# Loading half of the queries and keys through GpSimd's DMA queue, with the conversion to float16 on the way

## The chip, the core and the metric

The kernel runs on one core of one Trainium2 chip. The metric is the device time of one execution in microseconds (us); lower is better. TensorE (PE in the profile) multiplies matrices into PSUM; VectorE (DVE), ScalarE (ACT) and GpSimd (POOL) do the elementwise work; SyncE (SP) only issues transfers. ScalarE and GpSimd can issue transfers too. Each engine works through its own instructions in order and waits on semaphores for the others.

## The reference

Two layers follow each other. The first is attention with 4 batches, 8 heads, 768 positions and head size 64. A query sees the 8 first keys ("global") and the 96 last ones ("local"), with a bias that falls linearly with the distance:

```python
scores = scale * np.matmul(q, k.transpose(0, 1, 3, 2))
is_global = pos[None, :] < int(n_global)
is_local = (rel >= 0) & (rel < int(n_local))
bias = -slopes[:, None, None] * dist[None, :, :]
scores = np.where(is_global | is_local, scores + bias[None, :, :, :], -1000000000.0)
a = softmax(scores)                       # in short
return np.matmul(a, v).astype(np.float32)
```

Its output, 4 x 768 x 512, is the input x of the second layer: four attention experts of head size 64, causal, of which each position takes the best two by a gate.

```python
logits = x @ w_gate                       # the best 2 of 4 experts, softmax weights w
for e in range(E):
    q, k, v = x @ wq[e], x @ wk[e], x @ wv[e]
    a = softmax(causal(scale * (q @ k.transpose(0, 2, 1))))   # in short
    out += (w of e where e was chosen) * (a @ v @ wo[e])
```

All inputs and outputs are float32.

## The kernel before, in words

The 4 x 768 positions are cut into 24 row tiles of 128 positions: tile u is the rows u % 6 of batch u // 6. Everything is done per tile, in float16 on TensorE. There is no loop nest. A string `ORDER` near the end lists some 700 slots; a loop runs over them and calls one small function for each. So the order on every engine is written out by hand: an engine's own order is the order in which the slots come that give it work. A slot has a two-letter stage, a number (mostly the tile) and, where there is a choice, a letter for the engine or queue: `s` SyncE, `a` ScalarE, `g` GpSimd, `v` VectorE.

The slots that matter here:

- `lk`, `lq`, `lv` (function `load`, line 235; the transfer is L238): load tile u of k, q or v, 256 KB. The tile is [128 positions, 8 heads, 64], so memory is read in 128 x 8 runs of 64 float32, 256 bytes each. The buffers `kf`, `qf`, `vf` are float32, six of each.
- `kc`, `qc` (function `cast`, L258): convert a loaded tile to float16, into `s16k` or `s16q` (three buffers each).
- `vc`, `vx` (`cast_v`, L267): the same for values, in two parts, into the ring `vbuf`.
- `tk`, `tq` (`turn`, L283): TensorE transposes the four pairs of heads of the float16 tile into PSUM; L285 copies the result to `kqT`.
- `sa`, `sb` (`local_scores`, L345 and L352, exponentials at L355), `gs`, `gi` (global scores and keys), `va`, `vb` (`local_values`, L381): the first layer. `va` of tile u needs the values of tiles u and u - 1.
- `tx`, `pk`, `pq`, `pv` (L402, L414, L428): transposing and projecting the first layer's output.
- `ca`, `cb`, `cc` (L459, exponentials at L462), `ma` (`causal_mask`, L474, on GpSimd), `za`, `zb` (L487), `tz`, `ou` (`output`, L519 to L523): the second layer. `ro` is the choice of experts, small steps of which some are on GpSimd.
- `wm` (L248): multiplications without a use, [...].

Loads stand in `ORDER` well ahead of their casts. SyncE does hardly anything but issue them, so it reaches a load's slot early and then only waits for a free buffer, [...]. GpSimd reaches a slot when it has done all its earlier casts, masks and routing steps.

Of the kernel before, what the change touches and what calls it, by code (L numbers as in the profile page):

```python
# [8 lines left out]
F32 = mybir.dt.float32  # L9
F16 = mybir.dt.float16  # L10
# [8 lines left out]
P = 128  # L19
# [3 lines left out]
def kernel(  # L23
# [9 lines left out]
    V, S_, G = nc.vector, nc.scalar, nc.gpsimd  # L33
    dma = nc.sync.dma_start

    copies = {"a": S_.copy, "g": G.tensor_copy, "v": V.tensor_copy}
    queues = {"s": dma, "a": S_.dma_start}

    B, H, S, Dh = q.shape
    NT = S // P  # L40
    D = H * Dh
# [147 lines left out]
    raw = fast.enter_context(tc.tile_pool(name="raw", bufs=6))  # L189
    fast.enter_context(tc.manual_schedule())  # L190
    pp = fast.enter_context(tc.tile_pool(name="pp", bufs=3))
# [40 lines left out]
    fs, kqT, kgs, vgs, ags, xTs, kqs, lgs, wts, a2s, as_, done = ({} for _ in range(12))  # L232
    s16s, zs_, x16s, routing, zss, zts, tps, ppss, zs2 = ({} for _ in range(9))

    def load(u, nm, on):
        b, ri = divmod(u, NT)
        f = fs[nm, u] = raw.tile([P, H, Dh], F32, name=nm + "f")
        queues[on](f[:, :, :], {"k": k, "q": q, "v": v}[nm][b, :, ri * P:(ri + 1) * P, :]  # L238
                   .rearrange("h j d -> j h d"))

# [273 lines left out]
    def output(u, on):  # L514
        b, ri = divmod(u, NT)
        assert 3 in ready
        o_ps = psT.tile([P, D], F32, name="ops", tag="t")
        for ep in range(NEP):
            mm(o_ps[:, :], lhsT=zts[u][:, ep, :], rhs=wo16[:, ep, :],  # L519
               start=(ep == 0), stop=(ep == NEP - 1))  # L520
        o_sb = pp.tile([P, D], F32, name="osb", bufs=6)
        copies[on](o_sb[:, :], o_ps[:, :])
        dma(out[b, ri * P:(ri + 1) * P, :], o_sb[:, :])  # L523

# [220 lines left out]
    def branch_hint(_):  # L745
# [3 lines left out]

    stages = {  # L750
        "lk": (load, "k"), "lq": (load, "q"), "lv": (load, "v"),
        "kc": (cast, "k"), "qc": (cast, "q"), "vc": (cast_v, 0), "vx": (cast_v, 1),
        "wi": (weights_in,), "wc": (weights_cast,), "gi": (global_keys,),
# [7 lines left out]
        "ca": (causal_scores, 0), "cb": (causal_scores, 1), "cc": (causal_scores, 2),  # L761
        "ma": (causal_mask,), "za": (causal_values, 0), "zb": (causal_values, 1),
        "tz": (turn_z,), "ou": (output,), "ck": (check_sums,), "bh": (branch_hint,),
    }
    for slot in ORDER.split():
# [32 lines left out]
vx4g wi4s lv5s va3 vb3 lk7a ca0 ma0 pk2 pq2v tx3v ca1 vg4 va4 vb4 lq8s ca2 pk3 pq3a lk8s vc5v  # L798
vx5v cb2 vg5 wc2g lv6s kc7g lq9s pv0v pv1v lq10a lk9s qc7g qc8g kc8g ca3 cb3 tk7 lv7s tq7v pv2v
ro0 va5 sa6 tk8 tq8v tx4v vc6g vx6g lk10a lk11s vb5 sb6 gs4 lv8s ro0 pv3v pk4 qc9g pq4v ro0 ro0  # L800
lq11s lq12a ma1 vs1 lk12s lk13a sa7 tx5v kc9g pv4v kc10g ma2 vg6 va6 ro0 vb6 ca4 tk9 tq9v pk5
lk14s lq13s lv9a pq5v cb4 tx6v sb7 vc7v qc10g qc11a vx7g vc8g tk10 tq10v pv5v kc11g kc12g lq14a
qc12g cc4 vg7 va7 lq15s vb7 ro0 ro0 pk6 pq6a tk11 tq11v vx8g sa8 sb8 tx7v lk15s kc13g kc14g za0
qc13g zb0 lv10a tk12 tq12v gi2 pv6a sa9 sa10 ro1 ro1 lv11s lv12s vc9v vg8 va8 vb8 pk7 pq7a vx9g
tk13 tq13v lk16s lk17s gs5 ca5 qc14g lq16s tz0v za1 lq17s ro1 tk14 tq14v zb1 tx8a ro1 sb9 vc10g
vx10g sb10 kc15a pv7v pv8v vc11g vg9 va9 kc16a vb9 sa11 sa12 tz1v ro1 lq18s kc17v pk8 pq8a za2
ro1 tk15 zb2 sb11 sb12 qc15g tq15v tx9a vc12g vx11g vg10 va10 lk18s vx12g qc16g qc17v vb10 gs6
vs2 tk16 tq16v wi3s qc18g kc18g tk17 tq17v ma3 cb5 vg11 ma4 lk19s va11 lv13s lv14s cc5 tx10v
lv15s tk18 tq18v vb11 ca6 pv9v pv10a ro1 sa13 ro2 sa14 lq19s lq20s gi3 lq21s wc3g za3 ro2 zb3
ou0v ou1a vc13g ro2 ca7 lq22s ca8 vx13g vg12 ma5 va12 vb12 tx11v pk9 pq9v za4 ro2 lk20s kc19g  # L810
zb4 lk21s lk22s lv16s ma6 tz2a ro2 sb13 sa15 tx12v qc19v qc20g pk10 pq10a vc14g vx14g kc20g ma7
tz3v vg13 vc15g ro2 va13 vb13 lv17a cb8 gs7 ma8 ou2v tk19 tq19v lk23s lv18a za5 sb14 sb15 tz4v
zb5 tx13a pv11v sa16 ro2 sb16 vg14 va14 vb14 pk11 ro3 lv19s lv20a pq11a pv12v sa17 za6 zb6 ro3
ro3 vc16g vx15g vx16g ou3a ou4v qc21v ca9 lv21s cb9 tk20 kc21g tq20v za7 pk12 zb7 pq12a tx14v
vc17g ca10 vx17g ro3 cb10 vg15 va15 qc22g tz5v tz6v vb15 ou5a vc18g vc19g tk21 tq21v sa18 vc20v
sb17 kc22g kc23g za8 zb8 tx15a pk13 pq13v ca11 vg16 cc10 va16 pv13v lv22a pv14v cb11 ma9 vb16
gs8 ou6a pk14 pq14v ca12 vx18g vg17 va17 vb17 ca13 tz7v ro3 pk15 ro3 ro3 vx19v pq15a sb18 vs3
tx16v tx17v za9 zb9 ro4 pk16 lq23s pq16a ou7v ro4 lv23s qc23g cc11 vg18 va18 vc21g vb18 pv15a
tk22 tq22v sa19 sa20 ma10 pv16v ma11 za10 tz8a zb10 sb19 sb20 ro4 ro4 ro4 pv17v tz9v ca14 vg19
va19 vb19 ou8a ou9a vx20v sa21 sb21 ro4 ro4 tk23 tq23v ro5 za11 tx18v zb11 tz10a sa22 sb22  # L820
tx19v ma12 pv18v cb14 vg20 va20 vb20 gs9 ro5 ou10a pv19v ma13 vx21g ca15 ca16 vc22g za12 tz11v
zb12 pk17 pq17v pk18 pq18v ro5 ma14 ro5 vc23g cb15 vx22g vg21 va21 vb21 cb16 ro5 tx20v ro5 ro5
pk19 pq19a za13 zb13 pv20a ro6 sa23 sb23 tx21v vg22 va22 vb22 cc16 tz12v pk20 ro6 pq20a za14
zb14 ou11a ro6 ca17 ca18 tz13v ma15 za15 tz14v vx23g zb15 ro6 ro6 ou12a ou13v cb17 vg23 va23
vb23 cc17 ma16 tz15v pk21 pq21a za16 ro6 zb16 tx22v ro6 ca19 ca20 ma17 tx23v ma18 ma19 za17
tz16v zb17 ou14a pv21v cb20 ca21 za18 pv22v pv23v ro7 zb18 cb21 pk22 ro7 ro7 ro7 pq22a ma20
ma21 pk23 pq23a ro7 za19 zb19 ca22 ou15v tz17v cb22 za20 cc22 tz18v ro7 ro7 ou16a zb20 ou17v
ck0 ck1 ca23 bh0 cb23 za21 tz19v zb21 ou18v cc23 tz20v ma22 za22 zb22 tz21a ou19a ou20v ma23 za23 tz22v
zb23 ou21a ou22a tz23v ou23a ck2
"""  # L830

MAXB = 512
# [38 lines left out]
```

## Time and profile before

| what | value |
|---|---|
| time | 150.62 us, median of 2 runs (150.38 to 150.87) |
| span of the profiled execution | 150.8 us |
| TensorE clock granted | 0.998 |
| transfers | 27.77 MB, on two queues: SyncE's (q1) 21.51 MB, ScalarE's (q10) 5.77 MB |
| loads of q, k, v | 72 of 256 KB; median time from issue to landing 5.5 to 5.7 us on SyncE's queue, 4.5 to 4.9 us on ScalarE's |
| casts of q and k (L258) | GpSimd 32 (612 and 630 ns on the mean), DVE 9, ACT 7 |
| casts of v (L267) | GpSimd 76 (408 ns), DVE 20 (320 ns) |
| causal masks (L474) | GpSimd 48 (409 ns) |

The page gives the busy share of each engine over the whole span, then the span in 40 equal slices with one digit each, in tenths. A matmul's end is modelled, so a busy TensorE isn't always at its peak. Transfers are not counted as work of the engine that issues them. A timeline row gives start and duration in us, engine, line, operation, tiles, and in brackets how long the engine had been idle and what released it.

### The profile page before, as it was taken

The numbers are of one execution on the slowest core, as the hardware profiler recorded it, in microseconds if no ns is written. First come the engines' busy times: TensorE is split into PE (matmuls) and PEld (weight loads), VectorE is DVE, ScalarE is ACT, GpSimd is POOL, SyncE is SP. The second block draws the span as 40 slices with busy tenths as digits, with TensorE's granted clock in tenths as the row PEclk, the third lists the DMA queues.
The fourth block names the chain that finished last, engine by engine and source line by source line (L and its number), as shares of the span: only waits on it lengthen the run. The fifth ranks groups of instructions, "written<-read, shape, count | busy, mean of one in ns | idle before, by whom it ended". The sixth has DMA issues, their size and how long they took to land.

```text
span 150.8 us, 7217 instructions
## 1 busy us (share of the span) xinstructions
PE 140.3 (93%) x3029; PEld 110.2 (73%) x3029; DVE 111.4 (74%) x348; ACT 108.1 (72%) x176; POOL 90.2 (60%) x254
## 2 busy tenths in 40 slices
PE   5799999999999999999978999999999999999760
PEld 4567778887778888878757778888778878786520
DVE  4838676687899887878863987687787777778850
ACT  4027657778576888888638998887977978989640
POOL 7278351568878988797827899136286345463200
PEclk9999999999999999999999999999999999999999
DMA  4999998999999989899899963415221005013462
GB/s 99 280 252 286 276 261 192 254 247 238 277 282 275 245 201 249 189 256 208 231 240 288 301 166 113 116 43 142 74 77 70 4 19 195 24 51 127 155 263 97
DMA packets 85364, 27.77 MB, mean 184 GB/s; under 512 B 82000, under 2 KB 82000, under 8 KB 85328
## 3 DMA queue, kind: packets, MB, share of 16 engines
q1 hardware_dynamic: 62496, 21.51, 56.6%
q10 hardware_dynamic: 22832, 5.77, 17.1%
q8 instruction: 24, 0.39, 1.0%
q14 instruction: 12, 0.10, 0.2%
HBM read 20.98 MB, written 6.29 MB: 181 GB/s over the span
## 4 chain that ended last, share of the span: by engine, by line
PE 74%; DMA 11%; DVE 4%; POOL 3%; ACT 2%; issue 1%; SPq 1%; ACTq 0%; POOLq 0%; DVEq 0%
PE pps L414 14%; PE cps L459 7%; PE vps L428 7%; PE tp L283 7%; PE ops L519 6%; PE zps L487 6%; PE zps L381 6%; PE sps L345 5%; PE zps L248 4%; DMA kf<-in_k_dram 4%; DMA vf<-in_v_dram 4%; PE xps L402 3%; PE sps L352 3%; DMA qf<-in_q_dram 3%; PE zps L366 2%; PE ztps L509 2%
## 5 line engine op out<-in xcount | busy, mean ns | idle before, releaser
L462 ACT ACTIVATE a<-cps 128x1024 f16<-128x1024 f32 (+1 forms) x48 | 42.2, 917 | 8.3 <-PE cps L459 6.6
L355 ACT ACTIVATE abuf<-sps 128x636 f16<-128x636 f32 (+1 forms) x48 | 30.6, 686 | 12.8 <-PE sps L352 10.1
L267 POOL CAST vbuf<-vf 64x256 f16<-64x256 f32 x76 | 31.0, 408 | 8.4 <-DMA vf<-in_v_dram 5.2
L474 POOL TENSOR_SCALAR_AFFINE_SELECT a<-a 128x256 f16<-128x256 f16 x48 | 18.3, 409 | 5.1 <-ACT a L462 4.8
L285 DVE COPY kqT<-tp 128x1024 f16<-128x1024 f16 x23 | 15.7, 688 | 6.6 <-PE tp L283 6.1
L390 DVE TENSOR_TENSOR x<-zps,rinv 128x512 f16<-128x512 f32 x24 | 16.6, 691 | 0.8
L487 PE MATMUL zps<-v2buf,a 128*128 128x65 f16 x336 | 16.0, 193 | 0.6 <-DVE zs L498 0.5
L345 PE MATMUL sps<-biasT,ident 64*64 64x318 f16 (+1 forms) x192 | 14.5, 305 | 1.4 <-ACT abuf L355 1.3
L381 PE MATMUL zps<-vbuf,abuf 64*128 64x65 f16 x704 | 15.5, 189 | 0.0
L258 POOL CAST s16k<-kf 128x512 f16<-128x512 f32 x17 | 10.3, 612 | 8.7 <-DMA kf<-in_k_dram 8.3
L487 PEld LDWEIGHTS <-a 128*128 128x128 f16 x336 | 13.3, 97 | 2.1 <-DVE zs L498 0.9
L381 PEld LDWEIGHTS <-abuf 64*128 64x128 f16 x704 | 14.0, 94 | 1.1 <-issue 0.2
L414 PE MATMUL pps<-xT,wk 128*128 128x128 f16 x192 | 14.7, 219 | 0.0
L414 PE MATMUL pps<-xT,wq 128*128 128x128 f16 x192 | 14.5, 219 | 0.0
L248 PE MATMUL zps<-ident 128*128 128x240 f16 x75 | 12.8, 316 | 1.7 <-POOL ident masks.py:199 1.6
L428 PE MATMUL vps<-wvg,xT 128*128 128x260 f16 x96 | 13.9, 275 | 0.0
L459 PEld LDWEIGHTS <-kq 64*128 64x128 f16 x336 | 9.7, 94 | 5.8 <-issue 4.4
L459 PE MATMUL cps<-kq,kq 64*128 64x128 f16 x240 | 13.8, 218 | 0.0
L519 PE MATMUL ops<-wo,zt 128*128 128x512 f16 x48 | 13.5, 380 | 0.4 <-DVE zt L512 0.4
L352 PE MATMUL sps<-kqT 64*64 64x159 f16 (+2 forms) x384 | 13.8, 223 | 0.0
L258 POOL CAST s16q<-qf 128x512 f16<-128x512 f32 x15 | 9.4, 630 | 5.1 <-DMA qf<-in_q_dram 4.9
L414 PEld LDWEIGHTS <-wk 128*128 128x128 f16 x192 | 11.5, 98 | 0.8
(113 smaller groups left out, 286.4 us busy)
## 6 DMA issues: line engine op xcount, KB each, us to landing
out_dram<-osb SPq DMA_DIRECT2D x24, 256.0 KB, 2.3
qf<-in_q_dram SPq DMA_DIRECT2D x20, 256.0 KB, 5.6
kf<-in_k_dram SPq DMA_DIRECT2D x19, 256.0 KB, 5.7
vf<-in_v_dram SPq DMA_DIRECT2D x17, 256.0 KB, 5.5
vf<-in_v_dram ACTq DMA_DIRECT2D x7, 256.0 KB, 4.7
kf<-in_k_dram ACTq DMA_DIRECT2D x5, 256.0 KB, 4.9
qf<-in_q_dram ACTq DMA_DIRECT2D x4, 256.0 KB, 4.5
w<-in_moe_wk_dram ACTq DMA_DIRECT2D x1, 512.0 KB, 5.3
```

The costliest lines, as they stand in the source:

```text
L248: mm(current["z"][:, 0, 4 * P - 2 * NC:4 * P].rearrange("r (a n) -> r a n", a=2), lhsT=ident[:, :], rhs=ident[:, 0:NC].unsqueeze(1).to_bro ...
L258: copies[on](s16s[nm, u][:, :, :], fs[nm, u][:, :, :])
L267: copies[on](o[hf * KB:(hf + 1) * KB, c, :, 0:Dh], fs["v", u][c * KB:(c + 1) * KB, hf * HG:(hf + 1) * HG, :])
L345: mm(s_ps[o, hh, 0:2 * w].rearrange("r (c n) -> r c n", c=2), lhsT=ident2[r, :], rhs=biasT[r, p, 0:w].unsqueeze(1).to_broadcast([KB, 2, w] ...
L355: S_.activation(as_[u][:, :, g, :].rearrange("r h (c n) -> r h c n", c=2)[:, :, :, 0:w], s_ps[:, :, 0:2 * w].rearrange("r h (c n) -> r h c ...
L381: mm(zs_[u][:, hf, hq * VW:(hq + 1) * VW], lhsT=as_[u - prev][r, hq % 2, hq // 2, at:at + P], rhs=held("vbuf", u - prev)[r, c, hq, :], sta ...
L414: mm(p_ps[:, i, ep, :], lhsT=w[:, ko, ep, :, :].rearrange("r a d -> r (a d)"), rhs=xT[:, ko, :], start=(i == 0 and ep == 0 and ko == 0), s ...
L428: mm(v_ps[:, :], lhsT=xT[:, ko, :], rhs=wvg16[:, ko, :], start=(ko == 0), stop=(ko == NK - 1))
L459: mm(s_ps[:, e2, i, :], lhsT=kqs[b * NT + ci][r, 0, ep, :], rhs=kqs[u][r, 1, ep, :], start=(i == 0), stop=True, skip_group_check=True)
L462: S_.activation(a2[:, :, 4 * c:4 * c + len(part), :], s_ps[:, :, 0:len(part), :], func=Exp, scale=sc2)
L487: mm(z_ps[:, e, :], lhsT=a2[:, e % 2, (e // 2) * n + ci, :], rhs=held("v2buf", b * NT + ci)[:, e, :], start=(e == 0 and ci == 0), stop=Tru ...
L519: mm(o_ps[:, :], lhsT=zts[u][:, ep, :], rhs=wo16[:, ep, :], start=(ep == 0), stop=(ep == NEP - 1))
```

## The change

Queries and keys of tiles 12 to 23 are loaded by a transfer that GpSimd issues, into float16 buffers; the transfer converts. The casts `kc` and `qc` of these 12 tiles are deleted: 18 on GpSimd, 4 on DVE, 2 on ScalarE. The transposes then read the loaded tile itself. The load slots stay where they were in `ORDER`; only their letter changes, from `s` or `a` to `g`. The new buffers `kh` and `qh` are four of each, 1 KB a partition; to make room, the output buffers `osb` go from six to five. The purpose is to take the conversion off the engines. Loads of v, of tiles 0 to 11 and of the weights stay as they are.

```diff
-    queues = {"s": dma, "a": S_.dma_start}
+    queues = {"s": dma, "a": S_.dma_start, "g": G.dma_start}
...
     def load(u, nm, on):
         b, ri = divmod(u, NT)
-        f = fs[nm, u] = raw.tile([P, H, Dh], F32, name=nm + "f")
+        if on == "g":
+            f = s16s[nm, u] = raw.tile([P, H, Dh], F16, name=nm + "h", bufs=4)
+        else:
+            f = fs[nm, u] = raw.tile([P, H, Dh], F32, name=nm + "f")
...
-        o_sb = pp.tile([P, D], F32, name="osb", bufs=6)
+        o_sb = pp.tile([P, D], F32, name="osb", bufs=5)
```

In `ORDER`, a stretch as an example (tiles 15 to 18):

```diff
-vx10g sb10 kc15a pv7v pv8v vc11g vg9 va9 kc16a vb9 sa11 sa12 tz1v ro1 lq18s kc17v pk8 pq8a za2
-ro1 tk15 zb2 sb11 sb12 qc15g tq15v tx9a vc12g vx11g vg10 va10 lk18s vx12g qc16g qc17v vb10 gs6
-vs2 tk16 tq16v wi3s qc18g kc18g tk17 tq17v ma3 cb5 vg11 ma4 lk19s va11 lv13s lv14s cc5 tx10v
...
+ca5 lq16g tz0v za1 lq17g ro1 tk14 tq14v zb1 tx8a ro1 sb9 vc10g vx10g sb10 pv7v pv8v vc11g vg9
+va9 vb9 sa11 sa12 tz1v ro1 lq18g pk8 pq8a za2 ro1 tk15 zb2 sb11 sb12 tq15v tx9a vc12g vx11g
+vg10 va10 lk18g vx12g vb10 gs6 vs2 tk16 tq16v wi3s tk17 tq17v ma3 cb5 vg11 ma4 lk19g va11 lv13s
```

The moved loads stand in GpSimd's order like this: tile 12's q behind the first routing step of batch 0, then k of 12 and 13, k of 14, q of 13, q of 14 and 15, k of 15, k of 16 and 17 with q of 16 and 17, q of 18, k of 18, k of 19, q of 19 to 21, q of 22, k of 20 to 22, k of 23, and last q of 23, with value casts, masks and routing steps between them.

More of the change, by code (lines that the diff above doesn't have):

```diff
@@ L800 @@
 ro0 va5 sa6 tk8 tq8v tx4v vc6g vx6g lk10a lk11s vb5 sb6 gs4 lv8s ro0 pv3v pk4 qc9g pq4v ro0 ro0
[L801 to L805, printed above, removed]
@@ L806 @@
-vx10g sb10 kc15a pv7v pv8v vc11g vg9 va9 kc16a vb9 sa11 sa12 tz1v ro1 lq18s kc17v pk8 pq8a za2
-ro1 tk15 zb2 sb11 sb12 qc15g tq15v tx9a vc12g vx11g vg10 va10 lk18s vx12g qc16g qc17v vb10 gs6
-vs2 tk16 tq16v wi3s qc18g kc18g tk17 tq17v ma3 cb5 vg11 ma4 lk19s va11 lv13s lv14s cc5 tx10v
-lv15s tk18 tq18v vb11 ca6 pv9v pv10a ro1 sa13 ro2 sa14 lq19s lq20s gi3 lq21s wc3g za3 ro2 zb3
-ou0v ou1a vc13g ro2 ca7 lq22s ca8 vx13g vg12 ma5 va12 vb12 tx11v pk9 pq9v za4 ro2 lk20s kc19g
-zb4 lk21s lk22s lv16s ma6 tz2a ro2 sb13 sa15 tx12v qc19v qc20g pk10 pq10a vc14g vx14g kc20g ma7
@@ L812 @@
[L812 to L829, printed above, removed]
+lq11s lq12g ma1 vs1 lk12g lk13g sa7 tx5v kc9g pv4v kc10g ma2 vg6 va6 ro0 vb6 ca4 tk9 tq9v pk5
@@ new lines @@
+lk14g lq13g lv9a pq5v cb4 tx6v sb7 vc7v qc10g qc11a vx7g vc8g tk10 tq10v pv5v kc11g lq14g cc4
+vg7 va7 lq15g vb7 ro0 ro0 pk6 pq6a tk11 tq11v vx8g sa8 sb8 tx7v lk15g za0 zb0 lv10a tk12 tq12v
+gi2 pv6a sa9 sa10 ro1 ro1 lv11s lv12s vc9v vg8 va8 vb8 pk7 pq7a vx9g tk13 tq13v lk16g lk17g gs5
+ca5 lq16g tz0v za1 lq17g ro1 tk14 tq14v zb1 tx8a ro1 sb9 vc10g vx10g sb10 pv7v pv8v vc11g vg9
+va9 vb9 sa11 sa12 tz1v ro1 lq18g pk8 pq8a za2 ro1 tk15 zb2 sb11 sb12 tq15v tx9a vc12g vx11g
+vg10 va10 lk18g vx12g vb10 gs6 vs2 tk16 tq16v wi3s tk17 tq17v ma3 cb5 vg11 ma4 lk19g va11 lv13s
@@ new lines @@
+lv14s cc5 tx10v lv15s tk18 tq18v vb11 ca6 pv9v pv10a ro1 sa13 ro2 sa14 lq19g lq20g gi3 lq21g
+wc3g za3 ro2 zb3 ou0v ou1a vc13g ro2 ca7 lq22g ca8 vx13g vg12 ma5 va12 vb12 tx11v pk9 pq9v za4
+ro2 lk20g zb4 lk21g lk22g lv16s ma6 tz2a ro2 sb13 sa15 tx12v pk10 pq10a vc14g vx14g ma7 tz3v
+vg13 vc15g ro2 va13 vb13 lv17a cb8 gs7 ma8 ou2v tk19 tq19v lk23g lv18a za5 sb14 sb15 tz4v zb5
+tx13a pv11v sa16 ro2 sb16 vg14 va14 vb14 pk11 ro3 lv19s lv20a pq11a pv12v sa17 za6 zb6 ro3 ro3
+vc16g vx15g vx16g ou3a ou4v ca9 lv21s cb9 tk20 tq20v za7 pk12 zb7 pq12a tx14v vc17g ca10 vx17g
@@ new lines @@
+ro3 cb10 vg15 va15 tz5v tz6v vb15 ou5a vc18g vc19g tk21 tq21v sa18 vc20v sb17 za8 zb8 tx15a
+pk13 pq13v ca11 vg16 cc10 va16 pv13v lv22a pv14v cb11 ma9 vb16 gs8 ou6a pk14 pq14v ca12 vx18g
+vg17 va17 vb17 ca13 tz7v ro3 pk15 ro3 ro3 vx19v pq15a sb18 vs3 tx16v tx17v za9 zb9 ro4 pk16
+lq23g pq16a ou7v ro4 lv23s cc11 vg18 va18 vc21g vb18 pv15a tk22 tq22v sa19 sa20 ma10 pv16v ma11
+za10 tz8a zb10 sb19 sb20 ro4 ro4 ro4 pv17v tz9v ca14 vg19 va19 vb19 ou8a ou9a vx20v sa21 sb21
+ro4 ro4 tk23 tq23v ro5 za11 tx18v zb11 tz10a sa22 sb22 tx19v ma12 pv18v cb14 vg20 va20 vb20 gs9
@@ new lines @@
+ro5 ou10a pv19v ma13 vx21g ca15 ca16 vc22g za12 tz11v zb12 pk17 pq17v pk18 pq18v ro5 ma14 ro5
+vc23g cb15 vx22g vg21 va21 vb21 cb16 ro5 tx20v ro5 ro5 pk19 pq19a za13 zb13 pv20a ro6 sa23 sb23
+tx21v vg22 va22 vb22 cc16 tz12v pk20 ro6 pq20a za14 zb14 ou11a ro6 ca17 ca18 tz13v ma15 za15
+tz14v vx23g zb15 ro6 ro6 ou12a ou13v cb17 vg23 va23 vb23 cc17 ma16 tz15v pk21 pq21a za16 ro6
+zb16 tx22v ro6 ca19 ca20 ma17 tx23v ma18 ma19 za17 tz16v zb17 ou14a pv21v cb20 ca21 za18 pv22v
+pv23v ro7 zb18 cb21 pk22 ro7 ro7 ro7 pq22a ma20 ma21 pk23 pq23a ro7 za19 zb19 ca22 ou15v tz17v
@@ L830 @@
+cb22 za20 cc22 tz18v ro7 ro7 ou16a zb20 ou17v ck0 ck1 ca23 bh0 cb23 za21 tz19v zb21 ou18v cc23
+tz20v ma22 za22 zb22 tz21a ou19a ou20v ma23 za23 tz22v zb23 ou21a ou22a tz23v ou23a ck2
 """
```

## The prediction

> **What bounds the kernel now.** I read the page's engine shares first, then the busy time of each engine by stretch, then the timelines of GpSimd and TensorE around the loads that move.
>
> ```profile
> PE 140.3 (93%) x3029; PEld 110.2 (73%) x3029; DVE 111.4 (74%) x348; ACT 108.1 (72%) x176; POOL 90.2 (60%) x254
> ...
> POOL 7278351568878988797827899136286345463200
> ...
> DMA  4999998999999989899899963415221005013462
> ```
>
> TensorE (PE) is busy 93% of the span. GpSimd (POOL) looks free at 60%, but its row of 40 slices (3.8 us each) says otherwise: from about 40 to 92 us it stands mostly at 7 to 9. The DMA row stands at 8 or 9 up to 86 us.
>
> ```profile
> 50.00:60.00 10.00, 10.00 (x261) 8.32 (x263) 8.39 (x28) 8.75 (x16) 9.05 (x23) 1.00 1.00 226
> ...
> 70.00:80.00 10.00, 8.62 (x205) 7.03 (x203) 7.48 (x22) 5.79 (x11) 5.69 (x16) 1.00 1.01 241
> 80.00:90.00 10.00, 9.96 (x232) 7.77 (x232) 7.36 (x22) 8.68 (x14) 9.13 (x25) 1.00 1.01 258
> ```
>
> These are three stretches of 10 us (PE, PEld, DVE, ACT and POOL busy us). PE has no free time at 50 to 60 us; GpSimd has 0.95 us. The one hole of PE in mid-kernel is 10 - 8.62 = 1.38 us at 70 to 80 us. So **TensorE sets the time, and what can be gained is about 1.4 us**; what can be lost is whatever makes TensorE wait.
>
> One place shows how near the edge loads and GpSimd are: tile 18's keys. GpSimd's timeline there (start us, duration us, instruction, idle before and its releaser):
>
> ```profile
> 59.81 1.72 POOL L267 CAST vbuf<-vf 64x256 f16<-64x256 f32 x4
> 61.60 0.70 POOL L258 CAST s16q<-qf 128x512 f16<-128x512 f32 x1
> 62.91 0.61 POOL L258 CAST s16q<-qf 128x512 f16<-128x512 f32 x1 [0.62 <-DMA qf<-in_q_dram]
> 63.82 0.61 POOL L258 CAST s16k<-kf 128x512 f16<-128x512 f32 x1 [0.29 <-DMA kf<-in_k_dram]
> ```
>
> and, from TensorE's timeline (start, duration, instruction):
>
> ```profile
> 64.49 0.40 PE L283 MATMUL tp<-ident,s16k 128*128 128x128 f16 x4
> ```
>
> The load landed at 63.8, the cast ended at 64.43, the transpose (tk18) began at 64.49: no slack.
>
> [...]
>
> **The change part by part.** Tiles 12 to 23 have 24 loads of q and k.
>
> *Removed casts.* 24: 18 on GpSimd (one every 0.56 us where they follow each other: 10.1 us), 4 on DVE (about 0.45 us each, 1.8 us), 2 on ScalarE (0.63 us, 1.3 us). DVE and ScalarE run beside TensorE; they give nothing beyond the 1.4 us hole, which is partly a ScalarE wait.
>
> *Removed issues.* SyncE and ScalarE lose 24 loads, which [...] lets v loads go earlier. In before, ScalarE's own load at 78.20 waited for the q load that landed at 78.13, and its next activation idled 2.30 us, which made PE's 1.29 us wait. That can vanish: at most 1.4 us.
>
> *Added issues on GpSimd.* The unknown is X, GpSimd's time for one such issue, in order with its other work. Each load reads 128 x 8 = 1,024 runs of 256 B. **Lower bound:** 0.4 us, what one HWDGE issue takes on ScalarE's queue (0.37 to 0.45 us). [...] I take **X = 1.2 us**: [...] That size is a choice, the weakest number here.
>
> *Moved: when a load starts.* SyncE ran ahead of the compute; GpSimd issues a load only when its own work reaches that slot. Tile 18's keys were issued at 58.29 from SyncE. In the compiled order of the changed kernel they stand behind tile 12's first value casts and tile 11's, that is at 60.65 of before's clock. Ahead stand 13 other moved issues and 7 fewer casts (7 x 0.56 = 3.9 us), and two waits for loads fall away or are filled (1.09 and 0.30 us). GpSimd is done with this issue at 60.65 - 3.9 - 1.4 + 14X = 55.35 + 14X. Landing takes 3.2 us on an idle queue (the first load, 0.80 to 4.0) and 5.6 us in the median; I take 4.0. Needed at 64.49. **TensorE is late by 14X - 5.1**: 11.7 us at X = 1.2.
>
> *Moved: the value casts behind the issues.* Tile 15's second value cast ended at 85.61; PE first used that tile at 87.16, 1.55 us later. Up to there are 23 moved issues, 13 removed casts (7.3 us) and 6.9 us of waits that can be filled. **Late by 23X - 7.3 - 6.9 - 1.55 = 23X - 15.75**: 11.8 us at X = 1.2. The two demands are met by the same shift of TensorE, so the larger counts, not the sum. Causal masks and the key products for the global scores wait in the same queue with slack of 2 to 10 us; they add nothing beyond that.
>
> *New waits.* A moved load also waits for its buffer (four each for qh and kh), that is for the transpose four tiles earlier. Tile 17's keys wait for tile 13's transpose, at 52.8 in before, and GpSimd reaches that slot at about 53.4: nothing, as GpSimd is the later one. *Five output buffers instead of six:* an output copy waits for the store five back; that landed at 143.5 for the last copy (146.3): nothing.
>
> *After 92 us* GpSimd is below 60% busy and catches up, but the shift of TensorE stays, as TensorE has no free time to give back.
>
> Sum: 150.6 + 11.8 = **162.4 us**.
>
> **The rivals.**
> *(a) The issue is cheap, X at 0.4 to 0.5.* Then 14X - 5.1 is 0.5 to 1.9 us and 23X - 15.75 is negative; with the hole of 1.4 us gone, 149.7 to 152.5 us: not slower. For it: GpSimd is rid of 10 us of casts where it is fullest, and 24 x 0.42 is just that. [...]
> *(b) [...] X of 2 or more.* GpSimd becomes the bound from 40 to 92 us: at X = 2 late by 30.2, so 181 us; at X = 3, 204 us. For it: 1,024 runs on each side. Against: nothing in the trace; [...]
> *(c) The cast slows the DMA engines.* In before one load lands about every 0.95 us (landings at 69.14, 70.03; 73.19, 73.91, 74.81). If a converting load took twice that, 24 x 0.95 = 23 us more of a resource that is full up to 86 us; with PE's lead of some us, up to 20 us late, about 171 us by itself. For it: nothing but that no trace shows one.
>
> **How the numbers follow.** X between 0.6 and 1.6 or the DMA of (c): 0.52, 154 to 172 us; (b): 0.26; (a): 0.22, most of it within 2% of before (147.6 to 153.6). Range: from 150.5, which leaves out the better half of (a), to 186, where X = 2.2 (23 x 2.2 - 15.75 = 34.9), which leaves out the worst of (b). Over 2% faster would need 3 us, twice the hole: 0.05. Within 2%: 0.17. Slower: 0.78.
>
> **What would show it.** Right: GpSimd's queue shows 24 issues of about 1.2 us each; TensorE's first large wait is for a moved load, at tile 14 or 18, then for value casts of tiles 13 to 16; SyncE's v loads land well before their casts; after 100 us the timeline of before repeats, shifted by some 12 us. The step of X is wrong if an issue holds GpSimd for under 0.6 or over 1.8 us; the step of landing is wrong if a moved load takes over 6 us after its issue ends. The whole is wrong if TensorE waits less than 3 us more than before.

## The result, and the profile after

The changed kernel takes **166.14 us**, median of 2 runs (165.66 to 166.62), against 150.62 us before: a ratio of 1.103, with a 95% interval of 1.087 to 1.119. The profiled executions have spans of 164.8 and 150.8 us. (The ratios of this document compare only executions within 1.5% of the fastest of their kernel.) The profiled execution of the kernel before took 152.97 us. Its trace has a wait of TensorE of 1.29 us, from 78.16 to 79.45 us, which two variants of this kernel (below: value loads moved, 150.85 us, and a small load into 512 bytes, 152.25 us) don't have in theirs: read against it, delays after 79 us come out some 2 us too small. From the page of the changed kernel (engine shares, then the 40 slices, here of 4.1 us each):

```profile
PE 144.9 (88%) x3029; PEld 113.2 (69%) x3029; DVE 109.8 (67%) x344; ACT 107.5 (65%) x174; POOL 101.6 (62%) x260
...
PE   6799999999569998499986999999999999999820
...
POOL 7287326578999998986899388217268255462100
PEclk9999999999999999758997899999999999999995
DMA  5999999989999999779899954317331005105360
GB/s 118 275 247 282 278 204 207 242 183 282 224 205 252 205 203 74 50 51 74 175 136 182 179 159 127 72 68 95 72 131 68 4 0 195 42 28 189 130 263 8
```

TensorE's row now has gaps (5, 6 at 41 to 49 us, 4 at 66 to 70 us, 6 at 87 to 91 us), and two of them are followed by a fall of the granted clock (758, 78). TensorE works 4.6 us longer than before (144.9 against 140.3 us) at the same 3,029 matmuls, which goes with the lower clock (0.956 granted on the mean, before 0.998). By stretches of 10 us (busy us of TensorE, of its weight loads (PEld), DVE, ACT and POOL, then granted clock, DMA share, GB/s):

```profile
40.00:50.00 10.00, 6.66 (x133) 5.09 (x131) 6.46 (x15) 4.97 (x9) 9.62 (x19) 1.00 1.50 223
50.00:60.00 10.00, 9.94 (x249) 8.24 (x249) 7.92 (x25) 7.00 (x13) 9.54 (x18) 1.00 1.72 231
60.00:70.00 10.00, 7.25 (x187) 5.80 (x186) 4.91 (x17) 5.28 (x10) 8.76 (x22) 0.91 1.16 80
```

GpSimd has 0.4 and 0.5 us free in the first two stretches, and in the first and third it is fuller than TensorE. What fills it stands in the groups of instructions: the new issues, by line, tile and count, with busy us and mean ns.

```profile
L241 POOL DMA_DIRECT2D qh<-in_q_dram x12 | 11.2, 935 | 1.2 <-PE xps L405 0.5 <-PE cps L462 0.3 <-PE sps L355 0.3
L241 POOL DMA_DIRECT2D kh<-in_k_dram x12 | 10.9, 911 | 0.0
```

So an issue holds GpSimd for 0.92 us, 22.1 us in all; the 18 casts that left it had taken 0.61 to 0.63 us each, some 11 us. What TensorE waits for (us in total, times, longest):

```profile
PE vgps L307 <- POOL vbuf L270: 2.1, 1, 2.1
PE zps L490 <- DVE x L393: 2.0, 1, 2.0
PE tp L286 <- POOL s16k L261: 2.0, 2, 1.7
PE zps L251 <- POOL ident masks.py:199: 1.6, 1, 1.6
PE tp L286 <- POOL s16q L261: 1.6, 1, 1.6
```

The fourth row stands in the kernel before too (start-up). None of the others is for a moved load. Three are for casts that **stayed** on GpSimd (keys and queries of tiles 9 and 10, values of tile 12). The second, at 87.95 us, is put down to DVE, but DVE had itself stood 2.54 us for a routing step that GpSimd did behind three issues and two masks:

```profile
82.43 2.66 POOL L241 DMA_DIRECT2D kh<-in_k_dram  x3
...
86.45 0.21 POOL L554 TENSOR_TENSOR ex<-ex,d 128x12 f32<-128x12 f32 x1
```

```profile
86.70 0.17 DVE L557 TENSOR_REDUCE z<-ex 128x3 f32<-128x12 f32 x1 [2.54 <-POOL ex L554]
...
87.20 0.69 DVE L393 TENSOR_TENSOR x<-zps,rinv 128x512 f16<-128x512 f32 x1
```

```profile
87.95 0.54 PE L490 MATMUL zps<-v2buf,a 128*128 128x65 f16 x12 [2.05 <-DVE x L393]
```

The earliest wait is for tile 9's keys. In GpSimd's timeline (start, duration, instruction):

```profile
40.37 1.13 POOL L241 DMA_DIRECT2D qh<-in_q_dram  x1
41.51 0.79 POOL L477 TENSOR_SCALAR_AFFINE_SELECT a<-a 128x256 f16<-128x256 f16 x2
42.23 1.79 POOL L241 DMA_DIRECT2D kh<-in_k_dram  x2
44.01 1.19 POOL L261 CAST s16k<-kf 128x512 f16<-128x512 f32 x2
```

and in TensorE's:

```profile
44.70 0.40 PE L286 MATMUL tp<-ident,s16k 128*128 128x128 f16 x4 [1.73 <-POOL s16k L261]
```

Tile 9's key cast stands behind three issues (2.92 us). In the kernel before it ran at 40.48 and TensorE took the tile at 42.65. It starts 3.53 us later; 1.56 us of that was slack; the transpose is 2.05 us late. Comparing the two traces matmul by matmul, TensorE's delay then grows by 1.8 us at tile 10's queries, 1.2 at 65.9 us, 2.4 at tile 12's values, 2.4 while the clock is near a half, 0.6 at the cast of the output weights, 2.2 at 88 us and 0.8 at the second fall of the clock, which makes 13.3 us at 91 us. There the wait of the kernel before drops out, and 12.0 us are left at the last matmul; against the two variants without that wait it is 13.7 and 14.1 us. The last 2.0 us lie behind it: from the last matmul's end to the end of the program it is 6.42 us, before 4.43.

### The profile page after: what moved, and what is told of

The parts are those of the page before. It is cut to its first block, busy times and chain, and to the rows that moved or that the text cites. A ratio compares the mean times of both kernels' runs of the same rounds, so it can differ in the third digit from the quotient of the medians.

```text
span 164.8 us, 7185 instructions
## 1 busy us (share of the span) xinstructions
PE 144.9 (88%) x3029; PEld 113.2 (69%) x3029; DVE 109.8 (67%) x344; ACT 107.5 (65%) x174; POOL 101.6 (62%) x260
## 4 chain that ended last, share of the span: by engine, by line
PE 63%; POOL 10%; DMA 10%; DVE 6%; SPq 4%; issue 2%; ACT 1%; POOLq 0%; ACTq 0%; DVEq 0%
PE pps L417 9%; PE tp L286 6%; PE ops L522 6%; PE cps L462 6%; DMA vf<-in_v_dram 6%; PE zps L490 6%; PE vps L431 6%; PE zps L384 5%; PE sps L348 4%; DMA kf<-in_k_dram 4%; SPq L241 4%; PE zps L251 4%; PE sps L355 3%; POOL vbuf L270 3%; PE xps L405 3%
## 5 line engine op out<-in xcount | busy, mean ns | idle before, releaser
L490 PEld LDWEIGHTS <-a 128*128 128x128 f16 x336 | 13.7, 98 | 4.4 <-DVE x L393 2.2
L384 PEld LDWEIGHTS <-abuf 64*128 64x128 f16 x704 | 14.5, 95 | 1.3 <-issue 0.4
L431 PE MATMUL vps<-wvg,xT 128*128 128x260 f16 x96 | 14.4, 281 | 0.0
L355 PE MATMUL sps<-kqT 64*64 64x159 f16 (+2 forms) x384 | 14.3, 228 | 0.0
L355 PEld LDWEIGHTS <-kqT 64*64 64x64 f16 x384 | 11.4, 108 | 1.0 <-issue 0.2
L422 ACT CAST kq<-pps 128x512 f16<-128x512 f32 x16 | 9.3, 586 | 4.3 <-PE pps L417 4.2
```

The costliest lines, as they stand in the source:

```text
L355: mm(s_ps[o, hh, c * w:c * w + n], lhsT=kqT[b][r, 0, p, k0:k0 + KB], rhs=kqT[b][r, 1, p, k0:k0 + n], start=False, stop=True, skip_group_ch ...
L384: mm(zs_[u][:, hf, hq * VW:(hq + 1) * VW], lhsT=as_[u - prev][r, hq % 2, hq // 2, at:at + P], rhs=held("vbuf", u - prev)[r, c, hq, :], sta ...
L431: mm(v_ps[:, :], lhsT=xT[:, ko, :], rhs=wvg16[:, ko, :], start=(ko == 0), stop=(ko == NK - 1))
L490: mm(z_ps[:, e, :], lhsT=a2[:, e % 2, (e // 2) * n + ci, :], rhs=held("v2buf", b * NT + ci)[:, e, :], start=(e == 0 and ci == 0), stop=Tru ...
```

## The experiments

Each kernel was compared with runs of the kernel before on the same chip (medians 150.9 to 151.8 us there). Where a kernel of this section leaves the casts of tiles 12 to 23 out, its transposes read the upper halves of the float32 numbers, and a bound on the softmax factor is raised accordingly; the instructions on TensorE stay the same.

### What an issue costs alone

The first run has loads alone, in sizes of 128 to 2,048 runs, converting and plain.

> Not the reference's computation: a kernel of loads alone, one at a time on idle queues, each of seven forms three times: from GpSimd with conversion 128, 512, 1,024 and 2,048 runs of 256 B, from GpSimd 1,024 runs without conversion, from SyncE 1,024 runs, and from GpSimd with conversion 128 runs of 1,536 B; the output is filled with a few marks. The changed kernel's trace has 0.92 us of GpSimd for 1,024 converting runs. Theory 'mostly fixed': 0.7 to 0.9 us at 128 runs, at most 1.1 us at 2,048. Rival 'per run': about 0.11 us at 128 runs, 1.8 us at 2,048. Theory 'conversion is free for GpSimd': 0.9 us without conversion as well; rival: clearly less without. For the DMA engines: if conversion slows them, a converting load of 1,024 runs takes longer from issue to landing than the plain one from GpSimd, by 0.5 us or more.

Measured, GpSimd's time for one issue and time from issue to landing:

| load | issue, us | landing, us |
|---|---|---|
| 128 runs of 256 B, converting | 0.53 | 2.1 |
| 128 runs of 1,536 B, converting | 0.55 | 2.6 |
| 512 runs, converting | 0.75 | 2.7 |
| 1,024 runs, converting | 0.89 | 3.4 |
| 1,024 runs, plain | 0.89 | 3.5 |
| 2,048 runs, converting | 1.14 | 4.9 |

The issue has a fixed part of half a microsecond, less than the 0.7 to 0.9 us expected, and grows by 0.3 ns a run on the mean (more at first); the length of a run and conversion don't matter. Nor did conversion delay the landing of a load that ran alone (3.4 against 3.5 us). (A first execution of the smallest took 0.67.) The durations are only the engine's part: by the table, the landing came 1.6 to 3.8 us after the recorded end of the issue.

### Two false trails, and what they were

Two runs were to show the parts one by one. One adds to the kernel before a single small GpSimd load that nothing reads:

```diff
+    tiny = const.tile([P, 64], F16)
+    G.dma_start(tiny[:, :], k[0, 0, 0:P, :])
```

> The kernel before with one load more, 128 runs from GpSimd with conversion into a tile that nothing reads, at the very start. In the changed kernel's trace the stretch from the reading of the flag to the end is 2.0 us longer than before. Theory 'a fixed price of having used the GpSimd queue at all': this kernel pays it too, 152.1 to 153.1 us. Rival 'it comes from the 24 loads or from their late issue': 150.3 to 151.0 us.

Measured: 165.56 us (164.29 to 166.02), ratio 1.092 [1.082, 1.101]. The other puts 24 copies of 0.91 us on GpSimd in the slots of the moved loads, while the loads stay on SyncE and ScalarE and the casts are left out:

```diff
+    def busy(_):
+        G.tensor_copy(busy_out[:, :], busy_in[:, :])
```

> The kernel of the run without casts (same altered values), with one GpSimd copy of some 0.9 us on scratch data at each of the 24 load slots; the loads stay on SyncE and ScalarE. So GpSimd is as busy as in the changed kernel at the same places, while no load starts late, none converts and GpSimd issues none. Theory 'occupied GpSimd': TensorE stalls at tile 9 and 10's keys and at the values of tile 12 as in the changed kernel and its clock is halved for some us after, 159 to 164 us (the 12 us of shift seen in the trace, without the 2 us at the end). Rival 'late or slow loads': within 2 us of the kernel without casts.

Measured: four executions from 165.71 to 169.27 us. Each alone would explain the whole loss, which can't be. The second has no GpSimd load at all, and yet both have the same new mark, from the first microseconds on: transfers at some 220 GB/s. What they share are added tiles, which push all later tiles, those that the loads land in among them, to 128 and 64 bytes past a multiple of 512. The test is the kernel before with an unused tile and not one instruction more:

```diff
+    const.tile([P, 64], F16, name="pad")
```

> The kernel before with an unused SBUF tile of 128 bytes per partition ahead of the pools, so that every later tile moves up by 128 bytes and the instructions stay the same. Theory 'placement': the run with one small GpSimd load (165.6 us) and the run with busy slots (168.5 us) were slow because their added tiles moved the landing tiles of the loads off multiples of 512 bytes (to 128 and 64 past one), which capped the transfers at about 220 GB/s where the kernel before reaches 280. It expects 163 to 167 us here, with the GB/s row near 220 in the first 40 us. Theory 'software queue': the first GpSimd load is what slowed the hardware queues. It expects 150 to 152 us and a row near 280.

Measured: **162.49 us** (162.29 to 162.81), ratio 1.071 [1.065, 1.077]. Transfer rates in the 40 slices, of the kernel before and of this one:

```profile
GB/s 99 280 252 286 276 261 192 254 247 238 277 282 275 245 201 249 189 256 208 231 240 288 301 166 113 116 43 142 74 77 70 4 19 195 24 51 127 155 263 97
```

```profile
GB/s 115 223 218 218 222 218 182 231 211 197 221 231 224 220 219 207 225 187 246 219 256 233 222 265 241 106 128 21 126 134 5 65 4 110 96 65 68 157 248 131
```

In the second to sixth slices, 252 to 286 became 218 to 223. So the place of the tiles cost 7%. For the loads it is the writing side that moved; why that slows the transfers is not shown. The same small load with its tile made 512 bytes:

```diff
+    tiny = const.tile([P, 256], F16)
+    G.dma_start(tiny[:, 0:64], k[0, 0, 0:P, :])
```

> The kernel before with the one small unread GpSimd load again, its tile made 512 bytes per partition, so that all later tiles keep their place modulo 512. 'Placement' expects 150 to 152.5 us (at most the end of the program gets longer, by the 2 us between the last flag's read and the end that the changed kernel showed over the kernel before). 'Software queue' expects 164 to 167 us.

Measured: 152.12, 152.25, 154.79 and 154.82 us (before beside it 150.66 to 153.11). The 14 us are gone. In the trace the last matmul is no later than before, but the end of the program is 5.62 us behind it. In the run with the small load above it was 5.97 us; the kernels without a GpSimd load have 4.2 to 4.4. So one such load lengthens the end by 1.2 us or more. The change itself adds tiles of 1 KB and takes one of 2 KB away, all multiples of 512 bytes, and its rates in the second to fifth slices (247 to 282 GB/s, on its page above) are not those of the shifted kernel: placement is no part of its loss.

### GpSimd's time

First the removed casts alone: loads as before, casts of tiles 12 to 23 left out.

```diff
-kc15a ... kc16a ... kc17v ... qc15g
```

> The kernel before with the 24 casts of q and k of tiles 12 to 23 left out and nothing put in their place: loads stay on SyncE and ScalarE in float32, and the transposes read the upper halves of the float32 words as float16, so that the values are others and the bound on the reciprocal sums is widened. It shows what the removal is worth when it costs nothing. Theory 'TensorE sets the time': 148.5 to 150.8 us. Rival 'the casts were in the way': 147 us or less.

Measured: ratio 0.998 [0.995, 1.002] (150.06 to 155.22 us). Taking 24 casts away for nothing gains nothing. Now the busy slots again, with landing tiles on multiples of 512 bytes:

```diff
     busy_out = big.tile([P, 860], F16, name="busy_out")
+    big.tile([P, 224], F16, name="pad")
```

> The run without casts of tiles 12 to 23 and with 24 GpSimd copies of 0.9 us in the slots of the moved loads, as before, with a further tile of padding so that the landing tiles lie on multiples of 512 bytes again. Theory 'GpSimd's time': the issue time of the moved loads on GpSimd makes most of the loss; it expects 160 to 165 us, with TensorE waiting for GpSimd's casts of tiles 9 to 12. Theory 'landing': the converting transfers themselves and the end of the program make most of it; it expects under 155 us.

Measured: **160.92 us** (159.81 to 161.99), ratio 1.061 [1.052, 1.071]. GpSimd's timeline around tile 9's cast, and TensorE's waits in that run:

```profile
41.48 1.86 POOL L234 CAST busy_out<-busy_in 128x860 f16<-128x860 f32 x2
43.29 1.17 POOL L266 CAST s16k<-kf 128x512 f16<-128x512 f32 x2
```

```profile
PE zps L498 <- DVE x L401: 1.8, 1, 1.8
PE vgps L315 <- POOL vbuf L275: 1.7, 1, 1.7
PE tp L294 <- POOL s16q L266: 1.6, 1, 1.6
PE zps L256 <- POOL ident masks.py:199: 1.6, 1, 1.6
PE tp L294 <- POOL s16k L266: 1.4, 1, 1.4
```

They are the waits of the changed kernel, one for one, without a single GpSimd transfer. Then the same with 390 columns in place of 860:

```diff
-        G.tensor_copy(busy_out[:, :], busy_in[:, :])
+        G.tensor_copy(busy_out[:, 0:390], busy_in[:, 0:390])
```

> The run with 24 aligned busy slots on GpSimd, each copy cut from 860 to 390 columns, so from 0.91 us to some 0.42 us; landing tiles stay on multiples of 512 bytes. The forecast's slack sums (14X - 5.1, 23X - 15.75) are the theory 'slack': at X = 0.42 TensorE is late by 0.8 us, so 151.5 to 153 us, and a cheap issue would have cost next to nothing. Theory 'in proportion': every issue delays something TensorE waits for, and 0.42 / 0.91 of the 9.5 us between the run with 0.91 us slots and the one without casts is left: 155 to 157 us.

Measured: 153.05 us (152.42 to 153.91), ratio 1.013 [1.011, 1.016]. The slot turned out longer than meant:

```profile
L234 POOL CAST busy_out<-busy_in 128x390 f16<-128x390 f32 x24 | 12.2, 509 | 0.8
```

12.2 us in the slots in place of some 11 us of casts cost about 2 us; 21.8 us cost 9. The loss isn't in proportion: the first 12.2 us, about the time of the removed casts, cost little, and each further microsecond up to 21.8 us costs some 0.75. That is the theory of slack.

### The transfers themselves

The order of the changed kernel, loads on GpSimd's queue but unconverted, casts left out:

```diff
-        if on == "g":
-            f = s16s[nm, u] = raw.tile([P, H, Dh], F16, name=nm + "h", bufs=4)
-        else:
-            f = fs[nm, u] = raw.tile([P, H, Dh], F32, name=nm + "f")
+        f = fs[nm, u] = raw.tile([P, H, Dh], F32, name=nm + "f")
```

> The order of the changed kernel with the 24 moved loads on GpSimd's queue, but unconverted (float32 landing tiles, six of each as before), and no casts for tiles 12 to 23: their transposes read the upper halves of the float32 numbers, as in the run without casts. GpSimd's issue of 1,024 plain runs took 0.89 us by itself, as long as a converting one, so its time is the same as in the changed kernel; the transfers, though, take some 18 ns a packet of 256 bytes in place of 32 ns. Theory 'issue time and end': the run with busy slots (160.9 us) and the longer end (1.2 to 2.0 us) are all of the loss that is real; the landings count for nothing, and this is as slow as the changed kernel but for its half clock: 164 to 167 us. Theory 'landing': the slower converting packets hold up the value loads and so the casts; without them 161 to 163.5 us.

Measured: 164.98 us (163.31 to 166.82), ratio 1.089 [1.079, 1.098]. The queues of the changed kernel and of this one (packets, MB, share of 16 DMA engines):

```profile
q0 software_dynamic: 24960, 3.15, 30.1%
```

```profile
q0 software_dynamic: 1920, 6.29, 13.0%
```

Conversion does take the DMA engines longer: 32 ns for a packet of 128 bytes, where a plain packet of 256 bytes on the hardware queues takes 18 ns. Unconverted, GpSimd's loads went as 1,920 packets, 1,536 of them of 4,096 bytes, and took less than half the share for twice the bytes. Yet that changed the time by 1.2 us, within the two intervals. Against the busy slots the real loads cost 2.8% more even so, 4 us; 1.9 us of it is the end of the program (6.35 us behind the last matmul, 4.42 with the busy slots). The clock differs too: granted 0.957 on the mean here, 0.979 in the trace with busy slots.

### The clock

Fourteen idle matmuls more at each of two places of the changed kernel where TensorE had waited:

```diff
-vs2
+wm14 vs2
...
-za5
+wm14 za5
```

> The changed kernel with 14 more idle matmuls on TensorE ahead of the second selection of global values and ahead of the sixth causal values, where TensorE waited 2.1 us each and its granted clock then fell to about a half. Theory 'clock': some 4 us of the loss are TensorE at half clock after these two waits; it expects 162 to 163 us and no digit under 9 in the clock row there. Theory 'waits': the waits are what count and the work after them is late anyway; it expects 165.5 to 167 us.

Measured: ratio 1.076 [1.068, 1.084], from executions of 163.08, 163.34 and 165.50 us (two more took 166.21 and 167.49). The changed kernel and this one in the stretches after those waits:

```profile
68.00:72.00 4.00, 2.61 (x33) 2.34 (x34) 1.07 (x2) 0.74 (x2) 3.82 (x10) 0.53 0.54 37
72.00:76.00 4.00, 4.00 (x69) 3.34 (x64) 2.07 (x5) 2.65 (x3) 2.23 (x4) 0.62 1.47 94
88.00:92.00 4.00, 4.00 (x66) 2.99 (x70) 2.39 (x7) 1.88 (x3) 3.77 (x9) 0.59 1.45 225
```

```profile
48.00:52.00 4.00, 3.91 (x61) 3.19 (x62) 2.15 (x6) 0.60 (x1) 3.72 (x8) 0.57 1.56 222
68.00:72.00 4.00, 3.98 (x75) 3.39 (x75) 1.29 (x2) 1.46 (x4) 3.84 (x8) 1.00 0.61 41
72.00:76.00 4.00, 3.41 (x80) 2.65 (x79) 2.94 (x10) 3.47 (x6) 3.97 (x7) 1.00 1.32 84
88.00:92.00 4.00, 3.94 (x121) 3.25 (x119) 1.52 (x7) 2.81 (x5) 2.31 (x6) 1.00 1.33 223
```

The clock stays at 1.00 where it had been 0.53 to 0.62, but in this execution, of 165.50 us, it falls earlier instead, to 0.57 at 48 to 52 us. At full speed behind the first wait GpSimd's work comes earlier too, and the second wait ends at 86.42 us in place of 87.95. There the idle matmuls themselves stand in the way: they wait for the same step of DVE, and then take 1.59 us.

```profile
86.42 1.59 PE L251 MATMUL zps<-ident 128*128 128x240 f16 x14 [2.02 <-DVE x L393]
88.07 0.52 PE L490 MATMUL zps<-v2buf,a 128*128 128x65 f16 x12
```

At the last matmul 1.4 us are left. With the 1.6 us that the idle matmuls took, the clock is worth some 3 us by this pair of traces (an estimate); TensorE's delay had grown by 3.2 us (2.4 and 0.8) in the two stretches at half clock. The ratios differ by 2.7%, 4 us, with an uncertainty of nearly 3.

### Two ways out

The 24 issues at other places, two at a time, behind the transposes four tiles before (tiles 12 to 15) or three before:

```diff
+tq8v lk12g lq12g ... tq10v lk14g lq14g ... tq14v lk17g lq17g
```

> The changed kernel with its 24 GpSimd loads at other places of the order: keys and queries of a tile together, behind the transposes of the tile four before it (tiles 12 to 15) or three before it (16 to 23), so that no more than two issues stand in a row and the casts of tiles 9 to 11 come sooner. Theory 'bursts': the loss comes from runs of issues ahead of casts that TensorE needs at once; it expects 157 to 163 us, with the waits for GpSimd's casts of tiles 9, 10 and 12 together under half of their 6.2 us. Theory 'no room': GpSimd has no 22 us to give anywhere between 40 and 90 us, and each issue delays some cast; it expects 164 to 168 us.

Measured: 164.56 us (163.59 to 165.52), ratio 1.089 [1.082, 1.096]. TensorE's waits:

```profile
PE tp L286 <- POOL s16q L261: 3.3, 1, 3.3
PE vgps L307 <- POOL vbuf L270: 2.2, 2, 2.0
```

With 0.5 us for key casts, TensorE's waits for GpSimd's casts add up to 6.0 us; in the changed kernel they were 5.7. Tile 9's went, that for tile 10's queries doubled. This supports 'no room'; it was one other arrangement, not all.

The kernel before with three value loads moved from ScalarE's queue to SyncE's:

```diff
-lv17a ... lv18a ... lv20a
+lv17s ... lv18s ... lv20s
```

> The kernel before with the value loads of tiles 17, 18 and 20 moved from ScalarE's queue to SyncE's. The one part of the change that could help was to take loads off the engines; in the kernel before, ScalarE stands for some of these issues until a buffer is free. Theory 'worth little': removed waits on ScalarE lie beside TensorE's work; it expects 150.0 to 152 us, a ratio within 0.99 to 1.00. Theory 'hole': it takes away part of the one hole of TensorE at 70 to 80 us, and gives a ratio of 0.985 to 0.99.

Measured: 151.08 us, ratio 1.001 [0.998, 1.004]: worth nothing. No version was found that beats the kernel before.

## Why the prediction was right, and where its steps were off

**Direction and bound.** TensorE bounded the kernel, and the removed casts could give at most 1.4 us: the run without them gives 0.998 [0.995, 1.002], so in fact nothing. (The hole of 1.4 us is for the most part the wait at 78 us that the faster variants don't have.) GpSimd's queue, fullest from 40 to 92 us, is where the loss arose. Both as forecast.

**X, the time of one issue.** Taken as 1.2 us, measured 0.92 us, and 0.89 us alone. This term of the sum was 0.28 us too large. In the kernel, beside a DVE that was busy for 67% of the span, it was hardly longer than alone. The issue is a fixed half microsecond (0.53 us at 128 runs) and a part that grows with the runs (0.36 us more at 1,024). No trace of before has such an issue; the 1.2 us were the author's estimate.

**The delay, 14X - 5.1.** As a number it fits. At X = 0.51 it gives 2.0 us, and the run with short busy slots lost 1.3%, 2.0 us; at X = 0.91 it gives 7.6 us, measured 160.92 - 151.76 = 9.2 us. But the formula is the lateness of a moved load, with 4.0 us of landing in it, and in the runs with busy slots no load is moved. That it fits them is luck in part. The count in it is right: the 14 issues and 7 fewer casts also stand ahead of the second value cast of tile 12, which follows tile 18's key load in GpSimd's order, and there TensorE did wait:

```profile
67.57 0.88 POOL L241 DMA_DIRECT2D kh<-in_k_dram  x1
68.50 0.84 POOL L270 CAST vbuf<-vf 64x256 f16<-64x256 f32 x2
```

```profile
69.39 0.38 PE L307 MATMUL vgps<-vbuf,sel 64*64 64x65 f16 x7 [2.14 <-POOL vbuf L270]
```

In the kernel before this cast ended at 61.53 and TensorE took the values at 62.07. With this slack of 0.54 us in place of the landing, the forecast's own figures give 14X - 5.84 for the delay at this point (an estimate): 7.0, 6.9 and 1.3 us at X = 0.92, 0.91 and 0.51. The traces have 7.3 us in the changed kernel, 6.7 and 2.3 with busy slots.

**Where the delay is met: the step that failed.** "TensorE's first large wait is for a moved load, at tile 14 or 18": it never waits for a moved load. The forecast looked for the place where the most issues stand ahead and credited the removed casts. The first waits came at tiles 9 and 10, where three to five issues stand ahead and not one cast has been removed yet, and whose casts stay on GpSimd. When TensorE comes to tile 18's keys, at 73.54 us, it is 9.1 us late already and they have been there since 71.03. The later value casts (23X - 15.75, 5.4 us at 0.92) were the smaller demand. A wait that the forecast put at nothing was a large one: with "slack of 2 to 10 us" for masks and global keys, and no word on the routing steps, it left out the 2.0 us at 87.95.

**Landing.** Taken as 4.0 us from the end of the issue. The medians are 4.1 us (queries) and 5.5 us (keys), and 5 of the 24 loads are over the bound of 6 us, by up to 1.8. Too short, then, but without effect on TensorE; tile 18's own keys took 2.6 us. Nor were GpSimd's waits for value loads shorter: 5.6 us in all, before 5.2.

**After 92 us** the shift stays, as forecast: 12.2 us at 91.66 us and 12.0 us at the last matmul. Five output buffers cost nothing: in neither trace does a copy into one wait for a store.

**The sum.** With the measured X the forecast's own formula gives 150.6 + 7.8 = 158.4 us. It lacks 7.7 us: the end of the program (2.0), the formula's shortfall in the busy-slot run (1.6), and some 4 us of clock and landings. The clock is most of these: it cost 3.2 us in the trace of the changed kernel, of which the run with busy slots has 1.4 in its own trace already. The conversion is 1.2 at most by the medians. X too large by 0.28 us (14 x 0.28 = 3.9) made up half of that, so 162.4 came near 166.1 partly by luck, by two errors of opposite sign.

**The rivals.** (a) is right in its arithmetic: at an issue of 0.51 us the loss is 1.3%. The issue just isn't that cheap with 1,024 runs. (b) would need X of 2 us or more; at 2,048 runs it was 1.14. (c), conversion slowing the DMA engines: true of the packets (32 ns against 18), not of the time (166.1 converting, 165.0 plain).

Open: how much of the last 4 us is due to the real transfers as such. The run with idle matmuls is 1.5% (2.3 us) above the busy slots, and its longer end (6.83 against 4.42 us) alone would be 2.4, so little may be left for them; but a run with GpSimd's loads, a steady clock and no idle matmuls was not tried.

## What to carry to other kernels

Before moving a transfer to GpSimd to save casts, compare what goes with what comes in GpSimd's queue at the fullest stretch: here 18 casts of 0.62 us went and 24 issues of 0.92 us came, and the first deadline missed is that of the next work behind the first issues, not that of the data moved. Casts that run beside the bound may be worth nothing: here 24 were. When an experiment adds a tile, keep the landing tiles' place modulo 512 bytes and look at the transfer rate first, or the tile is what is measured: here 128 bytes more cost 7.1%, at 218 to 223 GB/s in place of 252 to 286, while a tile of 512 bytes left the rate at 260 to 289.

## What the runs showed of the hardware that wasn't expected

- An unused tile of 128 bytes made the unchanged instructions 7.1% slower: 256-byte packets of SyncE's and ScalarE's queues, from 4 to 20 us 18 ns each on the mean in the kernel before, took 24 to 25 ns there with the tiles 128 bytes further on. (Over the whole span, all packets of ScalarE's queue took 18.1 ns on the mean before and 23.4 ns there, from 17.1 and 20.8% of 16 engines' span.) In the first 4 us, with next to nothing on ScalarE's queue, they took 17.8 ns in either place.
- From the last matmul to the end of the program it took 4.2 to 4.4 us without a GpSimd transfer, 5.6 and 6.0 with one at the start of the program, and 6.4 us with the 24 of the change.
- The clock granted to TensorE in the changed kernel fell to 0.50 (0.53 to 0.62 on the mean of 4 us) in or behind single waits of 2.1 us. The falls began at 68.2 us, within the wait that ended at 69.39 us, and at 88.7 us, behind the one that ended at 87.95 us; in the 4 us before them TensorE was busy for 2.44 and 1.95 us. Behind the waits of 1.7 and 1.6 us that ended at 44.70 and 49.21 us it stayed at 1.00. What sets a fall off is not shown.
- A plain GpSimd load of 1,024 runs of 256 bytes went out in packets of 4,096 bytes (1,536 of them for 24 loads), the same load on a hardware queue in packets of 256 bytes.
